# Copies in program order, and turning transfers behind the x transfers, in a selective-attention and low-rank-mixer kernel

## The chip, the cores and the metric

The kernel runs on one core of one Trainium2 chip. The metric is the device time of one execution in microseconds (us). A core has five engines that run their own instruction streams: TensorE (PE, matrix products), VectorE (DVE), ScalarE (ACT), GpSimd (POOL) and SyncE (SP, which here only issues DMAs). They wait for each other by semaphores.

## The reference

Two layers are computed, for 8 batches of 576 positions: causal attention with a position bias from running sums (8 heads of 64 channels), and a mixer.

```python
scores = scale * np.matmul(q, k.transpose(0, 1, 3, 2))          # (8, 8, 576, 576)
cum = np.cumsum(np.maximum(s, 0.0), axis=-1)
bias = -(cum[:, :, :, None] - cum[:, :, None, :])
scores = np.where(causal, -1000000000.0, scores + np.minimum(bias, 0.0))
attn = softmax(scores)
x = np.matmul(attn, v)            # heads side by side: (8, 576, 512)
xt = x.transpose(0, 2, 1)
h = xt @ U @ V                    # rank 32
u = x + h.transpose(0, 2, 1)
out = u + np.maximum(u @ w_ch1, 0.0) @ w_ch2      # 512 -> 2048 -> 512
```

## The kernel before

**Pairs.** The unit of attention is a pair of heads. There are 32 pairs, four per batch: pair n belongs to batch n // 4. For each pair the kernel needs q and k with channels on the partitions. They lie in a slot of shape 128 x 2 x 1216 (rows 0 to 63 hold the channels, four more rows hold the running sums for the bias). From pair 8 on, three slots are used in turn.

**How q and k get into a slot.** For pairs 0 to 15 (batches 0 to 3) TensorE transposes them and VectorE or ScalarE copies them out of PSUM (`transposes`, L345 and L342). For pairs 16 to 31 (batches 4 to 7, `ZB` = 4) the work is split in three. `load_pairs(b)` lets POOL load the batch's q and k with positions on the partitions (L121). `turn_pair(n)` lets SP issue one transposing DMA that turns a pair's q and k into a landing place (L358). `part_pair(n)` lets SP load the four bias rows from HBM (L302), and VectorE copies the two heads out of the landing place into the two halves of the slot (L366, 64 x 1152 elements each). There are three landing places, used in turn: one tile named "turned" (pairs 16, 19, 22, 25, 28, 31) and the unused ends of the two q/k buffers, which bear the name "qk_sd" in the profile.

**Scores and values.** `scores(n)` multiplies q and k of a pair (L429), ScalarE takes the exponential (L447, L459, L465), VectorE masks (L373). `values(n)` multiplies with v (L493), and VectorE divides (L502, L503) into `x_sb`. From batch 2 on, behind the second head of a pair, SP issues a transposing DMA of the pair's x into `xT` (L510): the x transfer, 24 in all.

**Mixing.** `seqmix(b)` applies U and V to a batch's x. Its steps are: products with U (L522), a copy to `uxT` (L531), a transposing product (L535), a copy to `ux` (L537), products with V (L567, L592), and the evacuations of the accumulators, in which VectorE adds `xT` and writes `uT` (L547). The evacuation of each quarter of the channels needs the x transfer of one pair.

**The second layer** (`chanmix`) takes `uT` in groups of 512 positions: `hidden` (L662) and, from the second group on, products by quarters (L720) with sums on VectorE (L698, L734). It is traced as fill, a step at a time, between the steps of attention.

**Order.** The loop from pair 8 on runs over n, and traces in this order: `turn_pair(n + 3)`; a first step of `seqmix` where one is due (n = 4b + 1, for batch b - 1); `part_pair(n + 1)`; `scores(n)`; `values(n - 1)`; fill in between. What is traced is then planned: a planner orders each engine's instructions by their dependencies, an estimate of the times and the trace order. At the end, `in_program_order` fixes the trace order for POOL and TensorE in the whole kernel; for VectorE, ScalarE and SP it does so only up to the end of the first batch. Later instructions on these three stand where the planner puts them, except for single ones that the helper `placed` binds: it traces an instruction and makes it stand, on VectorE, behind the VectorE instruction traced just before it. Nothing is bound to stand behind the new instruction in turn.

Of the kernel before, what the change touches and what calls it, by code (L numbers as in the profile page):

```python
# [16 lines left out]
ALU = mybir.AluOpType  # L17


def in_program_order(tc, first, engines):  # L20

    traced, last = tc.nc.cur_bb.bb.instructions, {}
    for ins in list(traced)[first:]:
        if ins.engine not in engines:
            continue
        prev = last.get(ins.engine)
        if prev is not None:
            tc.add_manual_dep(
                ins,
                prev.name,  # L30
                mybir.DependencyInfo(
                    mybir.DependencyClass.NoSync, mybir.DependencyReason.DATA
                ),
                reason="in_program_order",
            )
        last[ins.engine] = ins


# [1 line left out]
def kernel(  # L40
# [12 lines left out]
    nc = tc.nc  # L53
    traced = len(nc.cur_bb.bb.instructions)
    E = mybir.EngineType
    B, H, S, D = q.shape
# [28 lines left out]
    def pwork():  # L85
        return ps_w.tile([128, 512], FP32, tag="w", name="pwork")
# [23 lines left out]
    def by_pairs(b):  # L110
        return qk_sd[b % 2][:TR, :QK].rearrange(
            "p (hp c t two d) -> p hp c t two d", hp=PB, c=2, t=RT, two=2
        )
# [62 lines left out]
    def v_slot(b):  # L176
        return v_slots[b % 3 if b < 3 else 2 - b % 2]
# [21 lines left out]
    def slot_of(n):  # L199
        return slots[n % NSLOT if n < 2 * PB else (n + 1) % 3]  # L200
# [50 lines left out]
    def weight_sums():  # L251
        for dst, a, b in ((B_1, B12, B11), (B_2, B22, B_1), (B_4, B21, B_2), (B_3, B22, B12)):
            for k4 in range(0, HF, 4):
                at = (slice(None), slice(k4, k4 + 4))
                traced = nc.cur_bb.bb.instructions
                before = max(i for i, ins in enumerate(traced) if ins.engine == E.DVE)
                nc.vector.tensor_sub(dst[at], a[at], b[at])
                in_program_order(tc, before, [E.DVE])
                yield
# [40 lines left out]
    def rows_of(n):  # L300
        for r, n_r, c in ((0, 3, 1), (3, 1, 0)):
            nc.sync.dma_start(  # L302
                out=slot_of(n)[ds(D + r, n_r), :, ds(c * S, S)],
                in_=rows_hbm[ds(r, n_r), ds(2 * n, 2)],
            )
# [47 lines left out]
    def landing(n):  # L353
        return landings[(n - ZB * PB) % 3]

    def turn_pair(n):
        b, hp = divmod(n, PB)
        nc.sync.dma_start_transpose(  # L358
            out=landing(n).rearrange("p (a m) -> p a m", m=TR),
            in_=by_pairs(b)[:, hp].rearrange("p c t two d -> p (c t two d)"),  # L360
        )

    def part_pair(n):
        rows_of(n)
        for hh in range(2):
            nc.vector.tensor_copy(slot_of(n)[0:D, hh, 0 : 2 * S], landing(n)[ds(hh * D, D)])  # L366
            yield

    def mask(dst, n_tiles, w, on_pool=False):
# [106 lines left out]
    def place(j, i):  # L476
        if i == j:
            return 128 * j if j < 4 else 1536
        return {0: 512, 1: 1024, 2: 1344, 3: 960}[j] + 128 * (i - j - 1)

    def values(n, pT):
        b, hp = divmod(n, PB)
        if hp == 0:
            x_of[b] = work.tile([128, PB, 5, 128], BF16, tag="x_sb", name="x_sb")
            if b >= FT:
                xT_of[b] = work.tile([128, 4, 640], BF16, tag="xT", name="xT", bufs=1)
        x_sb, vt = x_of[b], v_slot(b)
        for hh in range(2):
            h = 2 * hp + hh
            po = pwork()[:, : 5 * (D + 1)].rearrange("p (i d) -> p i d", i=5)  # L490
            for i in range(5):
                for j in range(i + 1):
                    nc.tensor.matmul(  # L493
                        po[:, i, :],
                        lhsT=pT[:, hh, ds(place(j, i), 128)],
                        rhs=vt[:, j, h, :],
                        start=(j == 0),
                        stop=(j == i),
                        skip_group_check=True,
                    )  # L500
            rec = work.tile([128, 5, 1], FP32, tag="rec", name="rec", bufs=4)
            nc.vector.reciprocal(rec, po[:, :, D : D + 1])  # L502
            nc.vector.tensor_tensor(  # L503
                x_sb[:, hp, :, ds(hh * D, D)],
                po[:, :, 0:D],
                rec.to_broadcast([128, 5, D]),
                op=ALU.mult,
            )
            if hh == 1 and b >= FT:
                nc.sync.dma_start_transpose(  # L510
                    out=xT_of[b][:, hp, :].rearrange("p (t m) -> p t m", t=5),
                    in_=x_sb[:, hp, :, :].rearrange("p t d -> p (t d)"),
                )
            yield


# [377 lines left out]
    def placed(ins_of):  # L894
        traced = nc.cur_bb.bb.instructions
        before = max(i for i, ins in enumerate(traced) if ins.engine == E.DVE)
        ins_of()
        in_program_order(tc, before, [E.DVE])
# [223 lines left out]
    M0, M1, M2, M3 = (mix_first(dt, act) for dt in range(PB))  # L1122
    A, B_ = (near_by_rows(hh, pT_of(0)) for hh in range(2))
    V0, V1, V2, V3 = (values(n, pT_of(n)) for n in range(PB))
    spin_some(9)
    step(T0)
# [66 lines left out]
    hidden_first(3)  # L1193
    mix_first_end()
    in_program_order(tc, traced, [E.DVE, E.Activation, E.SP])
    load_v(1)
    load_w2(1)
# [12 lines left out]
    def weave(order):  # L1210
        for word in order.split():
            if word == "F":
                fill_with(1)
                continue
            kind, n = word[0], int(word[1:])
            if word not in made:
                if kind == "T":
                    made[word] = transposes(n)
                elif kind == "S":
                    made[word] = scores(n, pT_of(n))  # L1220
                elif kind == "V":
                    made[word] = values(n, pT_of(n))
                else:
                    made[word] = seqmix(n)
            step(made[word])
            step_fill()
# [15 lines left out]
    for n in range(2 * PB, NP + 2):  # L1242
# [5 lines left out]
        if ZB * PB <= n + 3 < NP:  # L1248
            turn_pair(n + 3)
# [6 lines left out]
        if n > 2 * PB and n + 1 < NP:  # L1256
            for at, _ in enumerate((transposes if n + 1 < ZB * PB else part_pair)(n + 1)):
                step_fill()
                if at == 0:
                    step(mixing)  # L1260
# [10 lines left out]
        if 2 * PB < n <= NP:  # L1271
            run(values(n - 1, pT_of(n - 1)))
# [72 lines left out]
```

## Time and profile before

| what | value |
|---|---|
| runs without a profile | 356.35 us median of 3 (355.68 to 357.78) |
| profiled execution, its own time | 359.33 us |
| its span in the profile | 357.6 us |
| TensorE busy | 343.6 us, 96% of the span |
| VectorE busy | 264.4 us, 74% |
| ScalarE busy | 207.6 us, 58% |
| POOL busy | 112.6 us, 31% |
| granted TensorE clock | 1.00 |
| copies of L366 | 32: 20 out of qk_sd by 475 ns, 12 out of turned by 478 ns |

The span is the part of the execution that the profile covers; the profiled execution's own time also holds what lies around it. In a row of a timeline stand the start, the length, the engine, the line of the kernel, the operation, what it writes and reads with shapes, and the count; a bracket gives the engine's idle time before it and what ended that. "SPq" rows are DMA issues on SyncE's queue; their length is that of the issue and not of the transfer.

### The profile page before, as it was taken

What the parts mean: (1) busy time and instruction counts of PE and PEld (TensorE: products, weight loads), DVE (VectorE), ACT (ScalarE), POOL (GpSimd) and SP (SyncE); (2) the same over time, 40 slices, a digit from 0 to 9 for tenths busy, and PEclk for the clock granted to TensorE, in tenths of its full rate; (3) what the DMA queues carried; (4) which work ended last, traced back from release to release, by engine and by line L of the source; (5) the groups of instructions that cost most, each with busy time, mean ns of one, the idle gap of its engine ahead of it and who ended that gap; (6) DMA issues with size and microseconds to landing.
All of it is one profiled execution on the core that took longest, in us unless ns stands there. A gap on an engine that the chain in (4) does not pass through costs nothing.

```text
span 357.6 us, 9219 instructions
## 1 busy us (share of the span) xinstructions
PE 343.6 (96%) x3770; PEld 247.9 (69%) x3770; DVE 264.4 (74%) x584; ACT 207.6 (58%) x314; POOL 112.6 (31%) x158
## 2 busy tenths in 40 slices
PE   7999999999998999999999997899899999999996
PEld 3685656665587657775678565776588558888885
DVE  8686776779789849883798465983788779676774
ACT  4786965847762577348833874347752554675710
POOL 8897274447356603850366040000000000000000
PEclk9999999999999999999999999999999999999999
DMA  6999999999999999999599999472033525010022
GB/s 100 163 193 203 177 187 121 146 144 97 192 101 171 162 168 88 167 176 159 72 120 160 204 118 90 73 163 57 0 57 83 115 30 120 29 60 31 29 90 88
DMA packets 163713, 42.06 MB, mean 118 GB/s; under 512 B 148312, under 2 KB 162040, under 8 KB 163672
## 3 DMA queue, kind: packets, MB, share of 16 engines
q0 software_dynamic: 101744, 18.45, 80.7%
q1 hardware_dynamic: 61640, 22.83, 36.0%
q8 instruction: 29, 0.48, 0.6%
q10 hardware_dynamic: 288, 0.20, 0.2%
q14 instruction: 12, 0.10, 0.1%
HBM read 37.25 MB, written 9.70 MB: 131 GB/s over the span
## 4 chain that ended last, share of the span: by engine, by line
PE 77%; DVE 12%; ACT 5%; DMA 4%; issue 2%; POOL 0%; DVEq 0%; ACTq 0%; POOLq 0%
PE pwork L662 22%; PE pwork L720 12%; PE quarter L720 9%; PE pscore L429 9%; PE pwork L493 7%; PE parts L950 6%; PE pwork L681 3%; DVE uT L547 3%; DMA xT<-x_sb 2%; ACT pT L447 2%; PE pwork L322 2%; DVE slot L345 2%; DVE o_sb L734 2%; DVE slot L698 2%; ACT hT L1039 1%
## 5 line engine op out<-in xcount | busy, mean ns | idle before, releaser
L662 PE MATMUL pwork<-uT,w_sb 128*128 128x512 bf16 x432 | 106.6, 379 | 1.1 <-ACT hT L1039 0.9
L447 ACT ACTIVATE pT<-pscore 128x1024 bf16<-128x1024 f32 x56 | 56.5, 1031 | 52.7 <-PE pscore L429 52.3
L1039 ACT ACTIVATE hT<-pwork 128x512 bf16<-128x512 f32 x108 | 65.4, 610 | 37.1 <-PE pwork L662 36.3
L662 PEld LDWEIGHTS <-w_sb 128*128 128x128 bf16 x448 | 38.7, 98 | 38.0 <-issue 1.3
L429 PE MATMUL pscore<-slot 68*128 68x320 bf16 (+1 forms) x500 | 55.4, 246 | 0.6 <-ACT hT L447 0.3
L185 POOL DMA_DIRECT2D v_slot<-in_v_dram x40 | 33.8, 860 | 67.9 <-PE pwork L493 57.6
L429 PEld LDWEIGHTS <-slot 68*128 68x128 bf16 x564 | 41.8, 97 | 18.2 <-issue 1.2
L373 DVE TENSOR_TENSOR pT<-pT,keep 128x512 bf16<-128x512 bf16 (+1 forms) x81 | 28.5, 353 | 31.7 <-ACT pT L447 28.7
L720 PEld LDWEIGHTS <-hT 128*128 128x128 bf16 x496 | 46.7, 98 | 7.5 <-issue 0.8
L493 PEld LDWEIGHTS <-pT 128*128 128x128 bf16 x870 | 32.5, 97 | 10.2 <-issue 4.4
L493 PE MATMUL pwork<-v_slot,pT 128*128 128x65 bf16 x870 | 35.8, 193 | 3.8 <-DVE uT L547 3.1
L503 DVE TENSOR_TENSOR x_sb<-pwork,rec 128x320 bf16<-128x320 f32 x64 | 31.2, 489 | 1.5
L459 ACT ACTIVATE pT<-pscore 128x1024 bf16<-128x1024 f32 x29 | 30.4, 1047 | 2.6 <-PE pscore L429 2.4
L720 PE MATMUL pwork<-w_sb,hT 128*128 128x256 bf16 x240 | 30.1, 273 | 0.3 <-DVE o_sb L734 0.3
L345 DVE COPY slot<-pwork 64x576 bf16<-64x576 bf16 x30 | 24.1, 803 | 7.2 <-PE pwork L322 6.8
L121 POOL DMA_DIRECT2D qk_sd<-in_q_dram x32 | 23.8, 743 | 14.0 <-PE pwork L322 4.9
L720 PEld LDWEIGHTS <-slot 128*128 128x128 bf16 x256 | 24.1, 98 | 5.0 <-issue 1.9
L121 POOL DMA_DIRECT2D qk_sd<-in_k_dram x32 | 23.7, 740 | 5.7 <-DMA v_slot<-in_v_dram 1.8
L720 PE MATMUL pwork<-w_sum,slot 128*128 128x256 bf16 x160 | 20.1, 273 | 1.1 <-DVE o_sb L734 1.1
L720 PE MATMUL quarter<-w_sb,hT 128*128 128x256 bf16 x144 | 18.0, 273 | 0.3 <-DVE uT L547 0.3
L681 PE MATMUL pwork<-w_sb,hT 128*128 128x512 bf16 x64 | 16.3, 379 | 0.0
L502 DVE RECIPROCAL rec<-pwork 128x5 f32<-128x5 f32 x64 | 12.0, 189 | 5.4 <-PE pwork L493 5.0
(166 smaller groups left out, 513.7 us busy)
## 6 DMA issues: line engine op xcount, KB each, us to landing
out_dram<-o_sb SPq DMA_DIRECT2D x34, 256.0 KB
v_slot<-in_v_dram POOLq DMA_DIRECT2D x32, 128.0 KB, 7.7
w_sb<-in_moe_w_ch_dram POOLq DMA_DIRECT2D x4, 1024.0 KB, 13.3
qk_sd<-in_q_dram POOLq DMA_DIRECT2D x32, 72.0 KB, 6.0
qk_sd<-in_k_dram POOLq DMA_DIRECT2D x32, 72.0 KB, 5.9
qk_sd<-in_q_dram POOLq DMA_DIRECT2D x4, 288.0 KB, 12.4
qk_sd<-in_k_dram POOLq DMA_DIRECT2D x4, 288.0 KB, 11.5
qk_sd<-in_q_dram POOLq DMA_DIRECT2D x4, 144.0 KB, 5.2
```

Source lines behind the costliest of these rows:

```text
L121: nc.gpsimd.dma_start(out=by_pairs(b)[:, h // 2, c, :, h % 2, :], in_=src[b, h].rearrange("(t p) d -> p t d", p=TR),)
L185: nc.gpsimd.dma_start(out=vt[:rows_t, t, :, 0:D], in_=v[b, :, ds(t * 128, rows_t), :].rearrange("h p d -> p h d"),)
L345: copies(n, hh, par)(in_turn[:, :, :, :, par], src.rearrange("p c t m -> p c m t"))
L373: nc.vector.tensor_tensor(dst, dst, keep[:, :, 0:w].to_broadcast([128, n_tiles, w]), op=ALU.min)
L429: nc.tensor.matmul(dst, lhsT=slot[0:KA, hh, ds(S + j * 128, 128)], rhs=slot[0:KA, hh, lo:hi], start=True, stop=True,)
L447: nc.scalar.activation(pT[:, hh, 0:1024], near, EXP, scale=scale)
L459: nc.scalar.activation(pT[:, :, 1024:1536], mid.rearrange("p (a b) -> p a b", a=2), EXP, scale=scale)
L493: nc.tensor.matmul(po[:, i, :], lhsT=pT[:, hh, ds(place(j, i), 128)], rhs=vt[:, j, h, :], start=(j == 0), stop=(j == i), skip_group_check= ...
L503: nc.vector.tensor_tensor(x_sb[:, hp, :, ds(hh * D, D)], po[:, :, 0:D], rec.to_broadcast([128, 5, D]), op=ALU.mult,)
L662: nc.tensor.matmul(f1, lhsT=w1_sb[:, kt, ds(nf * 128, 128)], rhs=u[:, kt, :], start=(kt == 0), stop=(kt == 3),)
L720: nc.tensor.matmul(acc[:, i, :], lhsT=a[:, kt, ds(i * 128, 128)], rhs=b[:, kt, :], start=(begin and i == 0 and kt == 0), stop=(kt == HF - ...
L1039: nc.scalar.activation(hT[:, nf, :], f1, RELU)
```

## The change

Two orders are added; no instruction is added or taken away. The first: each of the copies out of a landing place is traced through `placed`, so that on VectorE it stands behind the instruction that is traced just before it. The second: each turning transfer stands, on SP, behind the latest x transfer that was traced before it. By the order of the loop, that is the x transfer of the pair five before the one that is turned. The helper `after` is the body of the loop in `in_program_order`, taken out.

```diff
+def after(tc, ins, prev):
+    tc.add_manual_dep(
+        ins,
+        prev.name,
+        mybir.DependencyInfo(mybir.DependencyClass.NoSync, mybir.DependencyReason.DATA),
+        reason="in_program_order",
+    )
...
+    x_turned = []
+
+    def last_sp():
+        return [ins for ins in list(nc.cur_bb.bb.instructions) if ins.engine == E.SP][-1]
+
     def turn_pair(n):
         b, hp = divmod(n, PB)
         nc.sync.dma_start_transpose(
             out=landing(n).rearrange("p (a m) -> p a m", m=TR),
             in_=by_pairs(b)[:, hp].rearrange("p c t two d -> p (c t two d)"),
         )
+        after(tc, last_sp(), x_turned[-1])
 
     def part_pair(n):
         rows_of(n)
         for hh in range(2):
-            nc.vector.tensor_copy(slot_of(n)[0:D, hh, 0 : 2 * S], landing(n)[ds(hh * D, D)])
+            placed(
+                lambda: nc.vector.tensor_copy(
+                    slot_of(n)[0:D, hh, 0 : 2 * S], landing(n)[ds(hh * D, D)]
+                )
+            )
             yield
...
                 nc.sync.dma_start_transpose(
                     out=xT_of[b][:, hp, :].rearrange("p (t m) -> p t m", t=5),
                     in_=x_sb[:, hp, :, :].rearrange("p t d -> p (t d)"),
                 )
+                x_turned.append(last_sp())
```

The lines of `placed`, which was there before:

```python
    def placed(ins_of):
        traced = nc.cur_bb.bb.instructions
        before = max(i for i, ins in enumerate(traced) if ins.engine == E.DVE)
        ins_of()
        in_program_order(tc, before, [E.DVE])
```

More of the change, by code (lines that the diff above doesn't have):

```diff
@@ L27, in in_program_order @@
         if prev is not None:
[L28 to L35, printed above, removed]
+            after(tc, ins, prev)
         last[ins.engine] = ins
```

## The prediction

> **What bounds the kernel now.** I read the page first, for who carries the chain, then TensorE's timeline for the places where it stands still, and then, for the largest of these, VectorE's timeline and SyncE's (SP's) queue.
>
> ```profile
> span 357.6 us, 9219 instructions
> PE 343.6 (96%) x3770; PEld 247.9 (69%) x3770; DVE 264.4 (74%) x584; ACT 207.6 (58%) x314; POOL 112.6 (31%) x158
> PE 77%; DVE 12%; ACT 5%; DMA 4%; issue 2%; POOL 0%; DVEq 0%; ACTq 0%; POOLq 0%
> ```
>
> TensorE is busy for 343.6 of 357.6 us. The change gives it no less to do, so it can win only from the 14 us in which TensorE idles. A DMA holds 4% of the chain, although no DMA should be on it. TensorE's timeline names the idle places near the edited code (start, length, group, and in brackets the idle time before it and who ended it):
>
> ```profile
> 112.82 0.29 PE L592 MATMUL pwork<-V_end,ux 128*128 128x64 bf16 x4 [0.28 <-DVE uT L547]
> 113.41 1.03 PE L720 MATMUL pwork<-w_sb,hT 128*128 128x256 bf16 x8 [0.30 <-DVE o_sb L734]
> 114.68 0.61 PE L493 MATMUL pwork<-v_slot,pT 128*128 128x65 bf16 x15 [0.24 <-DVE uT L547]
> ...
> 149.86 0.38 PE L720 MATMUL pwork<-w_sb,v_slot 128*128 128x256 bf16 x2 [0.30 <-DVE U L734]
> ...
> 184.87 0.29 PE L592 MATMUL pwork<-V_end,ux 128*128 128x64 bf16 x4 [0.35 <-DVE uT L547]
> 185.46 1.03 PE L720 MATMUL pwork<-w_sum,slot 128*128 128x256 bf16 x8 [0.30 <-DVE o_sb L734]
> ...
> 220.23 1.04 PE L720 MATMUL pwork<-w_sum,slot 128*128 128x256 bf16 x8
> 224.10 0.61 PE L493 MATMUL pwork<-v_slot,pT 128*128 128x65 bf16 x15 [2.83 <-DVE uT L547]
> 226.83 1.36 PE L720 MATMUL pwork<-w_sum,slot 128*128 128x256 bf16 x11 [0.78 <-DVE o_sb L734]
> ```
>
> All four places are mixing steps (seqmix), one per batch: batches 2, 3, 4 and 5. In each, TensorE waits for VectorE to empty accumulators into uT (L547). The idle times are 0.82, 0.30, 0.65 and 3.61 us, 5.38 in all. The fourth dwarfs the rest. Why it is longer is in VectorE's timeline and the chain in order of time (second fence line from the end):
>
> ```profile
> 219.28 0.75 DVE L547 TENSOR_TENSOR uT<-pwork,xT 128x192 bf16<-128x192 f32 x2
> 223.29 0.76 DVE L547 TENSOR_TENSOR uT<-pwork,xT 128x192 bf16<-128x192 f32 x2 [3.27 <-DMA xT<-x_sb]
> 226.10 0.68 DVE L734 TENSOR_TENSOR o_sb<-o_sb,pwork 128x512 f32<-128x512 f32 x1
> ...
> 214.58 8.62 DMA xT<-x_sb
> 212.34 0.48 DVE L503 TENSOR_TENSOR x_sb<-pwork,rec 128x320 bf16<-128x320 f32 x1
> ```
>
> VectorE stands 3.27 us because the last turning of x for this batch lands 8.62 us after its issue at 214.58. Its input was complete at 212.34 + 0.48 = 212.82. SP's queue shows what it stood behind:
>
> ```profile
> 208.78 1.42 SPq L510 DMA_TRANSPOSE xT<-x_sb  x1
> 210.30 1.33 SPq L302 DMA_DIRECT2D slot<-rows_hbm  x2
> 211.86 2.62 SPq L358 DMA_TRANSPOSE qk_sd<-qk_sd  x1
> 214.58 1.23 SPq L510 DMA_TRANSPOSE xT<-x_sb  x1
> ...
> L510 SPq DMA_TRANSPOSE xT<-x_sb x24: 1200/1254/2242, 94.1 to 282.1; - x24
> L358 SPq DMA_TRANSPOSE qk_sd<-qk_sd x10: 1307/2100/2847, 95.6 to 211.9; - x10
> L358 SPq DMA_TRANSPOSE turned<-qk_sd x6: 1279/1315/1413, 86.4 to 230.2; - x6
> ```
>
> The 24 transfers of L510 are those of pairs 8 to 31, the one at 214.58 the sixteenth, pair 23, the last of batch 5. The 16 of L358 are the turnings of pairs 16 to 31; landing places rotate by three, and the tile named "turned" takes 16, 19, 22, 25, 28 and 31. The turning at 211.86 comes after the fifth of these and is pair 30's. A turning wanted seven pairs later stands in front of a transfer that is wanted at once, and holds SP until 214.48.
>
> **The turnings.** In trace order iteration n traces turn_pair(n + 3) before values(n - 1), so the latest x transfer by then is that of pair n - 2: the turning of pair m now stands behind the x transfer of pair m - 5. That moves 28, 29 and 30 behind the transfers of 23, 24 and 25. The latest that may still stand ahead of pair 23's transfer is the turning of 27, allowed from 208.78 + 1.42 = 210.20 on. Its issue (1.3 us at its fastest) and the two row transfers (1.33) end at about 212.9, just when the input of pair 23's transfer is complete; so it is issued near 213, 1.6 us sooner, and with one turning less just ahead. When does it land? The nearest row without company is pair 27's:
>
> ```profile
> 247.85 1.78 SPq L510 DMA_TRANSPOSE xT<-x_sb  x1
> 251.00:252.00 1.00, 1.00 (x9) 0.59 (x7) 0.71 (x3) 1.00 (x2) 0.00 (x0) 1.00 0.00 0
> 210.97 4.21 POOL L185 DMA_DIRECT2D v_slot<-in_v_dram  x5 [14.32 <-PE pwork L493]
> ```
>
> The second line is the view by stretches; its last two columns are DMA share and GB/s. Both are zero from 251 on, so that transfer's data took 3.15 us at most. The bounds are 3.15 and 8.62 us after issue: 216.2 to 221.6. VectorE wants it at 219.28 + 0.75 = 220.03. I take a value between, some 5 us (218), because pair 30's turning is gone but the five loads of v that POOL issues from 210.97 stay; so the 3.27 us go. What is late next is VectorE's own run behind the evacuation: from 223.29 to the end of the addition at 226.78 are 3.49 us, so it would end at 223.5; TensorE, that starts again at 221.27 (220.23 + 1.04) instead of 224.10, would want that at 223.2 (as it does now at 226.05, where its 0.78 us begin). About 0.3 us of waiting stay: 3.61 - 0.34 = 3.27 us gained.
>
> The Trainium skill speaks against that: "DMA: Bandwidth & Descriptors", section "Issuing engines are not separate DMA queues", states that transfers of the SP, ACT and POOL queues run on the same 16 engines and interleave. By that alone the loads of v would keep the landing late, and the sum would be the second rival's.
>
> The price of the delay: a turning that is issued later must land before its copy. Copies of pair m are traced behind the VectorE work of values(m - 3), so between the two lie two pairs. The smallest distance is that of the x transfers of pairs 17 and 19, for the turning of 22 (the tenth and the twelfth of the 24):
>
> ```profile
> 165.88 2.14 SPq L510 DMA_TRANSPOSE xT<-x_sb  x1
> ...
> 176.98 1.23 SPq L510 DMA_TRANSPOSE xT<-x_sb  x1
> ```
>
> That is 11.1 us, against 2.14 of issue ahead plus at most 8.62 to land. It costs nothing; without that cover VectorE, and all masks and evacuations behind the copy, would wait for the landing. On SP, the rows, outputs and x transfers that a turning stood ahead of now go first, by its 1.3 to 2.8 us each; the turnings they delay have the 11.1 us.
>
> **The copies.** Nothing is added or removed: 32 copies by about 0.46 us, 15.2 us in all, move later. Today the planner puts them as soon as their slot is free, and in three of the four steps they stand directly ahead of the first evacuation, which begins within 0.05 us of their end, as the third step's does here at 182.86:
>
> ```profile
> 109.34 0.71 DVE L366 COPY slot<-turned 64x1152 bf16<-64x1152 bf16 x1
> 110.21 0.56 DVE L366 COPY slot<-turned 64x1152 bf16<-64x1152 bf16 x1
> ...
> 146.14 0.45 DVE L366 COPY slot<-qk_sd 64x1152 bf16<-64x1152 bf16 x1 [0.18 <-PE pwork L429]
> 146.77 0.46 DVE L366 COPY slot<-qk_sd 64x1152 bf16<-64x1152 bf16 x1
> ...
> 181.77 0.45 DVE L366 COPY slot<-qk_sd 64x1152 bf16<-64x1152 bf16 x1
> 182.38 0.46 DVE L366 COPY slot<-qk_sd 64x1152 bf16<-64x1152 bf16 x1
> 182.86 1.29 DVE L547 TENSOR_TENSOR uT<-pscore,xT 128x512 bf16<-128x512 f32 x2
> ...
> 209.03 0.94 DVE L366 COPY slot<-qk_sd 64x1152 bf16<-64x1152 bf16 x2 [0.58 <-PE pwork L429]
> ```
>
> They are the copies of pairs 16, 20 and 24 (the first, fifth and ninth of the sixteen pairs of copies), and in trace order belong to iterations 15, 19 and 23, two after the mixing steps (13, 17, 21). Gone from there, the evacuations can start up to 1.27, 0.91 and 0.91 us sooner; no more can come of it than TensorE's idle time, 0.82 + 0.30 + 0.65 = 1.77 us. At the low end it is nothing, or a loss: the steps of batches 3, 4 and 5 now hold the two copies of pairs 18, 22 and 26 near their start (0.94 us a step, as at 209.03), ahead of the chain from uxT over ux to the evacuation. Then 1.77 can shrink by 2 x 0.94 to -0.1. I take half, 0.9. The copies' wait for a slot ("PE pwork L429") goes too, but VectorE's idle time there is not on the path.
>
> **The sum.** 3.27 + 0.9 = 4.2 us. The profiled execution took 359.33 us, so it would take 355.1. The median of the runs shown is 2.98 lower, 356.35; I take the same loss of idle time from it: 352.2 us.
>
> **Rivals.** First, the turning of 27 takes the place of that of 30. Allowed at 210.20, it may be planned behind the rows, where 211.86 stands now; then pair 23's transfer is again issued at 214.58, lands at 223.2, and only the copies' 0.9 us are won: 355.4. For it: SP's order is the planner's, and the edit sets a lower end only. Against it: by trace order that turning comes before those rows. That the edits change next to nothing, because copies and turnings stay elsewhere in the order than meant, gives the same time. 0.17.
>
> Second, the loads of v alone are what delays the transfer. Issued at 213.0 and as slow as now, it lands at 221.6, 1.6 us after VectorE wants it: 3.27 - 1.6 + 0.9 = 2.6 us, 353.8. For it: POOL's issue at 210.97 falls into the same stretch. Against it: in the whole trace an evacuation waits for one landing only (row below), and the transfer at 176.98, the last of batch 4, was not waited for. The trace does not part the two causes. 0.18. This is the case by the skill's rule named above.
>
> ```profile
> DVE uT L547 <- DMA xT<-x_sb: 3.3, 1, 3.3
> ```
>
> Third, slower: the planner fills the freed place with sums. VectorE's order outside of the held copies is its own; a sum like that of L734 takes 0.68 us, and VectorE is nearly full in such a step (second line, third busy figure: 5.94 us of 6).
>
> ```profile
> L734 DVE TENSOR_TENSOR o_sb<-o_sb,pwork x20: 648/680/690, 104.5 to 276.3; 128x512 f32<-128x512 f32 x20
> 180.00:186.00 6.00, 5.35 (x53) 4.23 (x51) 5.94 (x16) 1.82 (x4) 4.00 (x6) 1.00 1.55 112
> ```
>
> If two more stand ahead of the awaited evacuation in each of the six mixing steps of batches 2 to 7, that is 12 x 0.68 = 8.2 us less the 4.2 won: 4.0 slower, 360.4. It decides from seven such sums on (4.8 > 4.2), and passes 0.5% from nine. For it: so full an engine hides nothing. Against it: the planner has the same work and fewer early copies to place. 0.18.
>
> **The numbers.** The forecast has 0.47. 0.5% is 1.78 us, about what a measurement of this kernel can tell from no change; within it lies 354.57 to 358.13. Faster are the forecast and the second rival, 0.65; the same is the first, 0.17; slower the third, 0.18. The low end takes all idle time of the four steps, 5.38 us: 351.0, less 0.6 for the spread of the runs, 350.4. The high end takes in the first rival with nothing won by the copies and the same spread, 357.0. The third rival is left out.
>
> **What would show it.** The turnings on SP alternate with x transfers, one behind each from pair 11 on; pair 23's transfer is issued near 213 and VectorE's 3.27 us at 223 are gone; TensorE's idle time before values in that step falls from 2.83 to under 0.3; no copy of L366 stands directly ahead of the evacuations of batches 2 to 4, and the first copies come two iterations later than at 109.34. I am wrong if a copy waits for a landing, if the transfer still lands after the evacuation of its neighbour, or if new idle time of over 1 us stands before scores (L429) or another mixing step.

## The result, and the profile after

The changed kernel takes 353.58 us (median of 6 runs, 353.48 to 353.75), the kernel before beside it 356.04 us (6 runs, 355.65 to 357.78). The ratio is 0.9924, with a 95% interval of 0.9903 to 0.9945: 2.5 us faster, where 4.2 were forecast. These six runs lie closer together than those before; 18 later runs of the changed kernel, shown below, lie between 353.44 and 355.05. The profiled execution took 353.70 us, against 359.33 before: between the two profiled executions the difference is 5.6 us, over twice that of the medians. Why is the main question of the experiments.

The page of the changed kernel, the three lines shown of before:

```profile
span 352.0 us, 9157 instructions
PE 340.9 (97%) x3735; PEld 248.1 (70%) x3770; DVE 263.9 (75%) x584; ACT 207.5 (59%) x314; POOL 112.9 (32%) x158
PE 80%; DVE 10%; ACT 5%; issue 3%; DMA 1%; POOL 0%; DVEq 0%; ACTq 0%; POOLq 0%
```

The DMA's share of the chain fell from 4% to 1%. TensorE's timeline at the four mixing steps (lines moved by 12 or 13 in the file: L493 is L505, L547 is L560, L567 is L580, L720 is L733; in the experiments below they move by up to as much):

```profile
111.83 0.28 PE L605 MATMUL pwork<-V_end,ux 128*128 128x64 bf16 x4
111.95 1.04 PE L733 MATMUL pwork<-w_sb,hT 128*128 128x256 bf16 x8
113.18 0.61 PE L505 MATMUL pwork<-v_slot,pT 128*128 128x65 bf16 x15 [0.19 <-DVE uT L560]
144.97 0.39 PE L580 MATMUL pscore<-V_sb,ux 32*128 32x512 bf16 x2 [0.51 <-DVE ux L550]
180.14 0.39 PE L580 MATMUL pscore<-V_sb,ux 32*128 32x512 bf16 x2 [0.48 <-DVE ux L550]
221.18 1.91 PE L733 MATMUL pwork<-w_sum,slot 128*128 128x256 bf16 x16 [0.41 <-DVE o_sb L747]
```

The idle times are 0.19, 0.51, 0.48 and 0.41 us, where they were 0.82, 0.30, 0.65 and 3.61. The first two rows had stops of 0.28 and 0.30 us before them and have none now. In batches 3 and 4 TensorE now waits at another place, for ux. SP's queue and VectorE around the step of batch 5:

```profile
203.54 1.23 SPq L522 DMA_TRANSPOSE xT<-x_sb  x1
204.96 1.30 SPq L365 DMA_TRANSPOSE qk_sd<-qk_sd  x1
206.91 0.90 SPq L304 DMA_DIRECT2D slot<-rows_hbm  x2
210.41 1.22 SPq L522 DMA_TRANSPOSE xT<-x_sb  x1
```

```profile
209.91 0.47 DVE L515 TENSOR_TENSOR x_sb<-pwork,rec 128x320 bf16<-128x320 f32 x1
...
216.99 1.41 DVE L560 TENSOR_TENSOR uT<-pwork,xT 128x192 bf16<-128x192 f32 x4
```

One turning stands between the x transfers of pairs 22 and 23. The latter is issued at 210.41, 0.03 us after its input is complete (209.91 + 0.47), and the four evacuations run without a break: the 3.27 us are gone. The copies, too, stand where the prediction put them. The first two are at 123.86, and in the mixing step of batch 3 one copy stands between uxT and ux:

```profile
123.86 0.91 DVE L375 COPY slot<-turned 64x1152 bf16<-64x1152 bf16 x2
...
141.31 0.81 DVE L375 COPY slot<-qk_sd 64x1152 bf16<-64x1152 bf16 x1
...
144.63 0.28 DVE L550 CAST ux<-pwork 128x128 bf16<-128x128 f32 x1
```

TensorE's order is the same in both kernels, so the same matmul can be used as a mark. Here the transposing product of uxT in the mixing steps of batches 2 to 6, before and then after:

```profile
107.74 0.22 PE L535 MATMUL pwork<-identity,uxT 128*128 128x128 bf16 x1
144.54 0.22 PE L535 MATMUL pwork<-identity,uxT 128*128 128x128 bf16 x1
179.88 0.22 PE L535 MATMUL pwork<-identity,uxT 128*128 128x128 bf16 x1
215.63 0.22 PE L535 MATMUL pwork<-identity,uxT 128*128 128x128 bf16 x1
250.88 0.22 PE L535 MATMUL pwork<-identity,uxT 128*128 128x128 bf16 x1
```

```profile
107.20 0.22 PE L548 MATMUL pwork<-identity,uxT 128*128 128x128 bf16 x1
142.87 0.22 PE L548 MATMUL pwork<-identity,uxT 128*128 128x128 bf16 x1
178.06 0.22 PE L548 MATMUL pwork<-identity,uxT 128*128 128x128 bf16 x1
213.34 0.22 PE L548 MATMUL pwork<-identity,uxT 128*128 128x128 bf16 x1
245.22 0.22 PE L548 MATMUL pwork<-identity,uxT 128*128 128x128 bf16 x1
```

The changed kernel leads by 0.54, 1.67, 1.82, 2.29 and 5.66 us at these marks. The 0.54 us at the first mark are no gain of the steps: in three more profiles in which the orders up to this mark are those of before, it stands at 107.03, 107.49 and 108.69. From mark to mark, 1.13 us are won in the stretch of batch 2's step, 0.15 in that of batch 3, 0.47 in that of batch 4, and 3.37 in that of batch 5.

### The profile page after: what moved, and what is told of

Its sections match the earlier page's. It is cut to its first block, busy times and chain, and to the rows that moved or that the text cites. A ratio compares the mean times of both kernels' runs of the same rounds, so it can differ in the third digit from the quotient of the medians.

```text
span 352.0 us, 9157 instructions
## 1 busy us (share of the span) xinstructions
PE 340.9 (97%) x3735; PEld 248.1 (70%) x3770; DVE 263.9 (75%) x584; ACT 207.5 (59%) x314; POOL 112.9 (32%) x158
## 4 chain that ended last, share of the span: by engine, by line
PE 80%; DVE 10%; ACT 5%; issue 3%; DMA 1%; POOL 0%; DVEq 0%; ACTq 0%; POOLq 0%
PE pwork L675 23%; PE pwork L733 13%; PE quarter L733 10%; PE pscore L441 9%; PE pwork L505 7%; PE parts L963 6%; PE pwork L694 3%; ACT pT L459 2%; DVE uT L560 2%; PE pwork L324 2%; DVE slot L347 2%; ACT hT L1052 2%; DVE slot L711 1%; PE pscore L402 1%; DMA qk_sd<-in_k_dram 1%
## 5 line engine op out<-in xcount | busy, mean ns | idle before, releaser
L675 PE MATMUL pwork<-uT,w_sb 128*128 128x512 bf16 x405 | 104.4, 379 | 2.5 <-ACT hT L1052 0.9
L733 PEld LDWEIGHTS <-hT 128*128 128x128 bf16 x496 | 46.6, 98 | 7.1 <-DVE uT L560 0.5
L505 PEld LDWEIGHTS <-pT 128*128 128x128 bf16 x870 | 32.6, 98 | 7.1 <-issue 1.3
L505 PE MATMUL pwork<-v_slot,pT 128*128 128x65 bf16 x870 | 36.1, 193 | 1.0 <-DVE slot L347 0.6
L733 PE MATMUL pwork<-w_sb,hT 128*128 128x256 bf16 x240 | 30.1, 273 | 0.0
L733 PEld LDWEIGHTS <-slot 128*128 128x128 bf16 x256 | 24.1, 98 | 4.3 <-issue 1.2
L733 PE MATMUL pwork<-w_sum,slot 128*128 128x256 bf16 x160 | 20.1, 273 | 0.4 <-DVE o_sb L747 0.4
L733 PE MATMUL quarter<-w_sb,hT 128*128 128x256 bf16 x144 | 18.0, 273 | 0.3 <-DVE uT L560 0.3
L976 DVE TENSOR_TENSOR hT<-pT,parts 128x512 bf16<-128x512 f32 x16 | 10.8, 684 | 6.3 <-PE parts L963 3.6
```

What stands on the lines that cost most here:

```text
L505: nc.tensor.matmul(po[:, i, :], lhsT=pT[:, hh, ds(place(j, i), 128)], rhs=vt[:, j, h, :], start=(j == 0), stop=(j == i), skip_group_check= ...
L675: nc.tensor.matmul(f1, lhsT=w1_sb[:, kt, ds(nf * 128, 128)], rhs=u[:, kt, :], start=(kt == 0), stop=(kt == 3),)
L733: nc.tensor.matmul(acc[:, i, :], lhsT=a[:, kt, ds(i * 128, 128)], rhs=b[:, kt, :], start=(begin and i == 0 and kt == 0), stop=(kt == HF - ...
```

## The experiments

**Is the wait always so long?** The kernel before, unchanged, was profiled again.

> The kernel before, unchanged, in another profiled execution. Theory: VectorE's wait for the x transfer of pair 23 (3.27 us in the execution shown) depends on how the transfers meet the loads of v and differs from execution to execution; the profile here shows 1 to 3.5 us of it, and the time is that of before within 0.3%. Rival: the wait is fixed, 3.2 to 3.4 us again, and the 2.98 us by which the profiled execution lay above the median come from elsewhere.

Time 356.91 us (355.36 to 359.98; ratio 1.0012, 0.9981 to 1.0043); profiled execution 357.81. VectorE's timeline at the step of batch 5:

```profile
221.78 0.76 DVE L547 TENSOR_TENSOR uT<-pwork,xT 128x192 bf16<-128x192 f32 x2 [2.14 <-DMA xT<-x_sb]
```

The wait is 2.14 us here and was 3.27 in the profile shown, in the same program. So it is no fixed cost. A third sample came by accident. The next edit was meant to move the last loads of v out of the transfer's way:

```diff
-        if hp == 0 and 2 <= b < B - 1:
+        if hp == (2 if b == 6 else 0) and 2 <= b < B - 1:
             load_v(b + 1)
```

> The kernel before, with the five loads of v for batch 7 issued two iterations later, so that they no longer meet the x transfer of pair 23; the turning of pair 30 stays ahead of it. Theory: the wait needs both, the turning ahead and the loads that slow it down; without the loads VectorE's wait (3.27 and 2.14 us in the two profiles of before) is under 0.5 us, and the runs lie together at 355.3 to 355.9 instead of spreading. Rival: the turning ahead is enough by itself; at least 1.5 us of the wait stay, 356 to 357.

These loads are POOL's last transfers and wait only for their place to be free, so a later place in the trace moves nothing: they were issued at 211.90, in the stretch of pair 23's transfer again. The time was 356.26 us (355.36 to 357.98; ratio 1.0002, 0.9978 to 1.0026), and these runs tell nothing of the loads. But it is one more profile of the same orders on all engines:

```profile
221.96 0.76 DVE L547 TENSOR_TENSOR uT<-pwork,xT 128x192 bf16<-128x192 f32 x2 [1.02 <-DMA xT<-x_sb]
...
211.90 4.21 POOL L185 DMA_DIRECT2D v_slot<-in_v_dram  x5 [15.59 <-PE pwork L493]
```

1.02, 2.14 and 3.27 us: this one wait differs by over 2 us from execution to execution, and the execution of the prediction had the longest of the three. Most of the difference is the time for which the turning of pair 30 holds SP. Its issue took 1.67, 1.95 and 2.62 us in these three profiles, and pair 23's transfer was issued 0.13, 1.11 and 1.76 us after its input was complete. It is not the whole: in the profile with 1.02 us the transfer was issued almost at once, at 213.87, and VectorE could go on only 8.1 us later.

**Do the loads matter?** This time they are left out.

```diff
-        if hp == 0 and 2 <= b < B - 1:
+        if hp == 0 and 2 <= b < B - 2:
             load_v(b + 1)
```

> The kernel before without the five loads of v for batch 7 (that batch's values are multiplied with the v of batch 5, which is left in the place); all other instructions and orders are the same, the turning of pair 30 stays ahead of pair 23's transfer. Theory: the wait needs the turning ahead and the loads that slow it down; without the loads VectorE's wait at the step of batch 5 (3.27, 2.14 and 1.02 us in three profiles of the same orders) is under 0.3 us, and the runs lie within 1 us at 355.0 to 355.7. Rival: the turning ahead is enough; 1 us of the wait or more stays, and the runs spread over 2 us as before.

355.64 us (355.24 to 356.36) against 356.35 for before on the same chip: ratio 0.9979, 0.9963 to 0.9996. VectorE at the step, and the marks of batches 2 and 6:

```profile
218.56 1.41 DVE L547 TENSOR_TENSOR uT<-pwork,xT 128x192 bf16<-128x192 f32 x4
...
107.03 0.22 PE L535 MATMUL pwork<-identity,uxT 128*128 128x128 bf16 x1
246.80 0.22 PE L535 MATMUL pwork<-identity,uxT 128*128 128x128 bf16 x1
```

The evacuations run through, although a turning stands ahead of pair 23's transfer as before. That turning's issue takes 1.31 us, the transfer is issued at 212.13, 0.03 us after its input is complete, and in the view by stretches nothing moves from 215 to 217: its data took 2.9 us at most, where the landing came 8.62 us after the issue in the profile shown. SP also came to this turning earlier here (2.32 us before that input, against 0.96), but with 2.9 us to land the transfer had some 4 us to spare. So the turning alone doesn't make the wait; it needs the loads of v beside it. The medians differ by 0.7 us (0.1 to 1.3 by the interval), which prices the loads, and with them the wait, in the usual run, the median. Between the two marks this kernel loses 139.77 - 138.02 = 1.75 us to the changed one. It has no wait in the step of batch 5, so this is the price of the early copies by themselves.

**Is it the turning of pair 30?** Only this turning is bound, and the copies are free.

```diff
+        if n == 30:
+            after(tc, last_sp(), x_turned[-1])
```

> The kernel before with one order more: the turning of pair 30 stands behind the x transfer of pair 25. Theory: it is this turning that makes pair 23's transfer late; VectorE's wait of 3.27 us is under 0.5, TensorE's idle time before values there under 0.5 instead of 2.83; the other idle places stay; 353.6 to 354.8 us. Rival (the loads of v delay the transfer whatever stands ahead): at least 1.6 us of the wait stay; 355.2 to 356.

In the profile the wait is gone, as the theory says, although the loads of v are there: the four evacuations run without a break from 219.02 on. But the time is 356.5 us (356.0 to 357.41; ratio 0.9998, 0.9985 to 1.0012): no gain, which neither the theory nor the rival has. VectorE's timeline and TensorE's show a new stop:

```profile
236.28 0.94 DVE L375 COPY slot<-qk_sd 64x1152 bf16<-64x1152 bf16 x2 [1.60 <-PE pwork L672]
...
238.16 1.04 PE L672 MATMUL pwork<-uT,w_sb 128*128 128x512 bf16 x4 [0.61 <-DVE x_sb L512]
```

The free copies of pair 30 now stand in VectorE's order ahead of the landing of their late turning: VectorE idles for 1.60 us and TensorE for 0.61 behind it. The profile puts that idle time down to a TensorE instruction; that it is the landing is concluded from the turning's issue at 232.49, under 4 us before. In the table further down this stop costs 0.78 us of the stretch, and the wait had cost the usual run some 0.7: it is concluded that the copy gives back what the order of the turning wins.

**The turnings' order alone.** All turnings bound, the copies free.

```diff
-            placed(
-                lambda: nc.vector.tensor_copy(
-                    slot_of(n)[0:D, hh, 0 : 2 * S], landing(n)[ds(hh * D, D)]
-                )
-            )
+            nc.vector.tensor_copy(slot_of(n)[0:D, hh, 0 : 2 * S], landing(n)[ds(hh * D, D)])
```

> Only the turnings are held behind the x transfers; the copies stay free. Theory: the planner still puts the copies of pairs 20 and 24 ahead of the evacuations of batches 3 and 4, and their turnings now come only behind the x transfers of pairs 15 and 19, 141.7 and 177 us on before's clock; a landing takes some 5 us, so VectorE waits about 3 us at each of the two steps: 0.5 to 5 us slower than before, 356.5 to 361. Rival: the turnings carry the whole gain, the copies wait for nothing: 353.6 to 354.6.

387.97 us (385.01 to 390.01): ratio 1.0876, 1.0835 to 1.0917. Right in kind, but 31 us against an expected 0.5 to 5. SP, VectorE and TensorE at the step of batch 2, and VectorE's waits for landings in all:

```profile
104.04 1.23 SPq L518 DMA_TRANSPOSE xT<-x_sb  x1
105.50 2.19 SPq L365 DMA_TRANSPOSE turned<-qk_sd  x1
...
114.45 0.45 DVE L374 COPY slot<-turned 64x1152 bf16<-64x1152 bf16 x1 [5.62 <-DMA turned<-qk_sd]
...
117.54 0.40 PE L601 MATMUL pwork<-V_end,ux 128*128 128x64 bf16 x4 [5.53 <-DVE uT L556]
...
DVE slot L374 <- DMA qk_sd<-qk_sd: 22.5, 8, 6.4
DVE slot L374 <- DMA turned<-qk_sd: 9.6, 4, 5.6
```

The copy of pair 16 stands ahead of the evacuations, and its turning comes only behind the last x transfer of that same batch. VectorE waits 5.62 us with everything queued behind it, and TensorE stops for 5.53. It happens in every batch and not at two steps: twelve waits, 32.1 us. That the planner has the landings earlier, by its estimate, than they come is concluded from where it puts the copies.

**The copies' order alone.**

```diff
-        after(tc, last_sp(), x_turned[-1])
```

> Only the copies are held; the turnings stay free. Theory: a turning needs its landing place, which a held copy frees later, so that holding the copies alone moves the turnings of 29 and 30 behind the x transfer of pair 23: as fast as the changed kernel, 353.2 to 354.2. Rival: the two orders share the gain, and without the turnings' own order pair 23's transfer is late again: 355 to 356.

354.36 us (353.71 to 355.02), ratio 0.9938, 0.9917 to 0.9958. That is just above the 353.2 to 354.2 expected, and the interval overlaps with that of the changed kernel. TensorE's idle places in the steps are those of the changed kernel, the same 0.51, 0.48 and 0.41 us among them, and SP's queue is this:

```profile
204.39 1.23 SPq L521 DMA_TRANSPOSE xT<-x_sb  x1
205.84 1.30 SPq L365 DMA_TRANSPOSE turned<-qk_sd  x1
207.74 0.89 SPq L304 DMA_DIRECT2D slot<-rows_hbm  x2
211.24 1.27 SPq L521 DMA_TRANSPOSE xT<-x_sb  x1
```

Again one turning stands between the two x transfers; now it is pair 28's. A landing place is free only when its copy is done, and so held copies hold the turnings too. In the steps the copies' order carries the change. What the turnings' own order adds the runs do not settle (ratios 0.9938 and 0.9924, with overlapping intervals), but the profiles show a place ahead of the steps at which it counts:

```profile
86.84 1.36 SPq L365 DMA_TRANSPOSE turned<-qk_sd  x1
93.28 0.60 SPq L304 DMA_DIRECT2D slot<-rows_hbm  x1
97.50 0.60 PE L439 MATMUL pscore<-slot 68*128 68x128 bf16 x6 [0.58 <-DMA slot<-rows_hbm]
```

This is the profile of the last version below, whose turnings are free. The turning of pair 16, the first, stands ahead of bias rows that TensorE wants at 97. In the changed kernel these rows are issued at 81.43, as that turning comes only at 105.50. Of nine profiles with this turning free, four have the wait (1.40, 0.16, 0.58 and 0.58 us; the 1.40 in the third sample of before's orders above); of the five with all turnings bound, none has it.

**The steps, stretch by stretch.** The same marks in these kernels' profiles give the time of each batch's stretch, in us:

| kernel | profiles | batch 2 | batch 3 | batch 4 | batch 5 |
|---|---|---|---|---|---|
| before, with the third sample | 3 | 36.67 to 36.80 | 35.34 to 35.35 | 35.74 to 35.75 | 35.25, 34.12, 32.99 |
| without the last loads of v | 1 | 36.79 | 35.34 | 35.75 | 31.89 |
| turning of pair 30 bound alone | 1 | 36.67 | 35.34 | 35.74 | 32.67 |
| copies held, turnings free | 1 | 35.66 | 35.19 | 35.27 | 31.89 |
| changed kernel | 3 | 35.65 to 35.67 | 35.19 to 35.20 | 35.27, 35.28, 36.16 | 31.88 |

The gain in batches 2, 3 and 4 hardly varies and comes with the held copies alone. What varies is batch 5's stretch before the change, and it goes with the wait of 3.27, 2.14 or 1.02 us. The 36.16 has a wait of its own, shown below.

**Can the copies' new cost be saved?** The wait for ux in batches 3 and 4 (0.51 and 0.48 us) comes from the second copy of pairs 18 and 22, held between uxT and ux. Two ways to get rid of it were tried. In the first, the second copy is traced behind the evacuations of the step:

```diff
-            for at, _ in enumerate((transposes if n + 1 < ZB * PB else part_pair)(n + 1)):
+            parted = (transposes if n + 1 < ZB * PB else part_pair)(n + 1)
+            for at, _ in enumerate(parted):
                 step_fill()
                 if at == 0:
                     step(mixing)
+                    if hp == 1 and n + 1 >= ZB * PB:
+                        step_fill()
+                        break
...
         for _ in mixing:
             fill_with(1)
+        if n > 2 * PB and n + 1 < NP:
+            drain(parted)
```

> The changed kernel, with the second copy of pairs 18, 22, 26 and 30 traced behind the evacuations of the mixing step instead of between uxT and ux; TensorE's order is the same. Theory: that copy makes ux late in batches 3 and 4, and TensorE's 0.51 and 0.48 us before L580 go: 352.3 to 353.1 us. Rival: VectorE is full there, and the copy costs the same behind the evacuations: 353.3 to 353.9.

353.38 us (352.93 to 354.25; ratio 0.9921, 0.9889 to 0.9952), against 353.83 for the changed kernel on the same chip, and not the 352.3 to 353.1 of the theory. The same without the turnings' order:

> As the second kernel of this call, but without the order of the turnings. Theory: held copies free the landing places late enough to order the turnings by themselves; the time is that of the second kernel within 0.5 us. Rival: the turnings' own order is worth something in the runs, and the time is 0.6 to 1.0 us above it.

353.63 us (353.1 to 354.41; ratio 0.9921, 0.9896 to 0.9946): no difference that the runs can tell from the first. In its profile the first shows no wait for ux any more, but one that the changed kernel did not have, at the first matmuls behind the step of batch 3:

```profile
157.59 1.02 PE L675 MATMUL pwork<-uT,w_sb 128*128 128x512 bf16 x4 [0.51 <-DVE o_sb L747]
```

In batch 3 the copy costs the same a little later, as the rival has it: the stretch takes 35.40 and 35.52 us in the two versions, against 35.20. In batch 4 it does not: there the second version takes 34.72 us against 35.28, while the first has a wait of 0.6 us for an x transfer. The changed kernel itself was run again beside them:

> The changed kernel unchanged, as the standard for the others of this call: 353.3 to 353.9 us, with no wait for an x transfer in the profile.

353.83 us (353.44 to 355.05). Its profile has one wait for an x transfer after all, in the step of batch 4. On SP two row transfers stand just ahead of that x transfer and a turning just behind it, at 178.46; POOL issues the five loads of batch 6's v from 174.02 on:

```profile
184.76 1.08 DVE L560 TENSOR_TENSOR uT<-pwork,xT 128x256 bf16<-128x256 f32 x3 [1.01 <-DMA xT<-x_sb]
```

In the second way, all copies are held but those of pairs 18, 22, 26 and 30, and the turnings are free:

```diff
-            placed(
-                lambda: nc.vector.tensor_copy(...)
-            )
+            copy = lambda: nc.vector.tensor_copy(...)
+            copy() if n % PB == 2 else placed(copy)
...
-        after(tc, last_sp(), x_turned[-1])
```

> The copies are held except those of pairs 18, 22, 26 and 30, which the planner may place early; the turnings are free. Theory: these four pairs of copies then lie in VectorE's gaps before the mixing steps, as in the kernel before, and neither ux (0.51 and 0.48 us) nor the step of batch 5 waits: 352.4 to 353.2 us. Rival: VectorE's work near the steps stays the same and the waits only move: 353.3 to 354.0.

353.25 us (352.96 to 354.12; ratio 0.9919, 0.9893 to 0.9944). Between the stop of 0.19 us at 113.48 and that of 0.41 at 220.74 TensorE has no idle time of 0.05 us or more in its profile. The version was run once more beside the changed kernel:

> The kernel that holds all copies but those of pairs 18, 22, 26 and 30 and leaves the turnings free, again, beside the changed kernel on the same chip. Theory: it saves the 0.75 us of TensorE's time that its first profile showed against the changed kernel's: 0.4 to 0.9 us below the next kernel of this call. Rival: the saving drowns in the runs' spread: within 0.3 us of it.

> The changed kernel, unchanged, as the standard beside the one above: 353.4 to 354.0 us.

353.65 us (353.19 to 354.35; ratio 0.993, 0.9906 to 0.9954) against 353.81 (353.44 to 354.07; ratio 0.9932, 0.9911 to 0.9954). The waits for ux are gone in both profiles, and the stretches of batches 2, 3 and 4 are 0.7 us shorter in all than in the changed kernel (35.80, 34.73 and 34.87 us in the first). But the runs do not show this version to be faster. The second profile has the wait for the rows at 97.50, and its stretch of batch 1, ahead of those in the table, takes 38.25 us where the changed kernel's takes 37.52. That free turnings give the gain back there in the usual run is likely and not shown; these copies with the turnings bound were not tried.

## Why the prediction was right or wrong

**Direction and mechanism: right.** The turning of pair 30 had stood ahead of pair 23's transfer, which is now issued as soon as its input is there. The evacuations run through, the wait of 0.41 us that stays is about the 0.34 foretold, and no copy waits for a landing. That the time fell within the stated range is in part luck: the two terms were wrong in opposite directions.

**The turnings' term was mis-sized.** The step that failed is "I take the same loss of idle time from it", which carries a gain of one execution over to the median. In the two profiled executions the step of batch 5 gave 3.37 us, against 3.27 forecast. But the wait is different in every execution (3.27, 2.14 and 1.02 us in three profiles), and the usual run seems to have less of it than any of the three: without the loads of v the median falls by 0.7 us (0.1 to 1.3). The warning was in the numbers: the profiled execution lay 2.98 us above the median, nearly as much as the whole wait.

**The copies' term was mis-sized the other way.** 0.9 us were forecast from a range of -0.1 to 1.77; the stretches of batches 2, 3 and 4 gave 1.13 + 0.15 + 0.47 = 1.75, and the kernel without the wait confirms that sum, as do the stretches of the table. The loss named for the low end is there: the second copy delays ux by half a microsecond in batches 3 and 4. But the same stretches gain more than the idle rows of the steps add up to. "No more can come of it than TensorE's idle time" was wrong: the idle time in a bracket is not all that a stop costs. Without stops a row begins before the modelled end of the row ahead of it: after the change the row at 111.83 follows one that starts at 110.09 and takes 1.91 us, so it begins 0.17 us early. With a stop this overlap is lost too. From 0.54 us at the mark the changed kernel's lead grows to 0.99 at the row of 112.82 in the kernel before, and to 1.46 at that of 113.41: the stops of 0.28 and 0.30 us cost 0.45 and 0.47. Together with 0.04 at the third stop that is 0.96 of the 1.13; the rest comes in small pieces further on. One reading was loose as well: not all of these stops wait for uT (L547). Of the 5.38 us of the four steps, 1.68 end with the sums of L734, the 0.30 of batch 3 among them.

1.75 and 0.7 make 2.45 us, and 2.46 were measured; the agreement is closer than the interval of the 0.7 allows to claim.

**"It costs nothing", of the later turnings:** right only together with the held copies. The prediction treated the two edits as separate gains. In the steps they are one: held copies delay the turnings by themselves, and delayed turnings without held copies cost 31 us. What the turnings' order gains by itself lies ahead of the steps, at the rows: the prediction saw them go first and counted no gain for it.

**Rivals.** The second came nearest in time, 353.8 us, and its cause was half right: it said that the loads of v alone delay the transfer. Without the loads there is no wait, so they are needed. But with pair 30's turning out of the way the wait is gone in the profiles of batch 5's step with the loads in place, so both are. The rule of the Trainium skill named for it ("DMA: Bandwidth & Descriptors", section "Issuing engines are not separate DMA queues") is that DMAs run on the same 16 DMA engines and interleave, whichever engine started them. The trace agrees: pair 23's transfer landed 8.62 us after its issue beside POOL's loads and took 2.9 us at most without them. The wait of 1.01 us in one of three profiles of the changed kernel also met loads of v, and a turning just behind; which of the two made it was not tried. The first rival did not come about: the turning of 27 was planned ahead of the rows. Nor did the third: the kernel is not slower.

## What to carry to other kernels

A profile is one execution: before a wait for a DMA is booked as a gain, compare the profiled time with the median, and profile the same kernel again, because a wait that depends on how transfers meet can be a fraction of that in the usual run. When a transfer is moved later on purpose, hold its reader in the order too; an in-order engine whose planned reader comes too early stops with everything behind it. An idle time in a bracket is no upper bound of what removing the stop can win. And look for orders that follow from others: here, holding the readers freed the landing places later, and thereby put the transfers of the steps in order with no edge on the queue.

## What was not expected of the hardware

Copies of the same shape take very different times. VectorE's copies out of the landing places in the changed kernel, least, median and most in ns:

```profile
L375 DVE COPY slot<-qk_sd x20: 411/455/831, 131.3 to 243.1; 64x1152 bf16<-64x1152 bf16 x20
```

All copies over 0.5 us stand in stretches in which POOL issues loads, but so does one of 0.41, at 139.07; whether that is the cause was not tried.
